# Key loads ahead of the weights, two clamps on VectorE, and the last tokens' product at the end of kv's accumulation

## The chip, the core and the metric

The kernel runs on one core of a Trainium2 chip. The metric is the device time of one execution in microseconds (us). Before the change it is 1074.74 us, the median of three runs (1074.12 to 1076.08). The engines have short names: PE is TensorE (matmuls; PEld its weight loads), DVE is VectorE, ACT is ScalarE, POOL is GpSimd, and SP only issues transfers. Each engine works through its own instructions strictly in the order in which they were written to it.

## The reference

An attention with random features, and a feed-forward product over its output:

```python
q_s, k_s = (q * scale, k * scale)
def phi(x):
    h = einsum('bhsd,md->bhsm', x, omega) - sum(x * x) / 2.0
    return np.exp(h - max(h)) / np.sqrt(m)
q_p, k_p = (phi(q_s), phi(k_s))
kv = einsum('bhsm,bhsd->bhmd', k_p, v);  z = sum(k_p, axis=2)
attn = einsum('bhsm,bhmd->bhsd', q_p, kv) / (einsum('bhsm,bhm->bhs', q_p, z) + 1e-06)
x = attn, heads side by side              # 4608 tokens x 512
h = x @ w_in                              # 512 x 2048
out = (h - np.tanh(h)) @ w_out            # 2048 x 512
```

There are 8 batches, 8 heads, 576 tokens, a head size of 64 and 128 features.

## The kernel before

**Units.** The heads go in four pairs c (0 to 3). A *k unit* (b, c) turns the keys of batch b into features and sums them with the values to `kv` and z. A *q unit* (ch, c) turns a chunk of 256 tokens of queries into the transposed attention output x. Batches 0 and 1 and chunks 0 to 2 are done "native" in f32, with tiles of the pool a0; this is the first stage. A native `k_unit` loads `kf` (keys) and `v` (values) through SP, lets POOL copy the last 64 tokens of both heads into the diagonal blocks `kd` and `vd` (L186, L187), and makes features on PE (L160, L196), their smallest exponents on DVE (L162, L197) and the exponentials on ACT (L164, L198). Then PE accumulates kv in `pk`: first the product of the last tokens (`ph`, `vd`, L201), then eight products over the other 512 tokens (L205). z goes to DVE (L212) and, transposed, to `zb`, which the q units read.

**Weights.** `w` holds both weight matrices as f64 words, in 16 slices f of 1 MB. `fetch` loads a slice into `raw`; `decode` splits it into two fp32r parts: absolute value on ACT (L437), a middle word `m` on ACT (L439), a clamp on POOL (L440), bit work on DVE (L442, L443, L446), the high part on ACT (L450), and two more DVE operations (L451, L452) that give `w`. The tile `a` has two buffers and `m` one, so the `m` of a slice waits for L452 of the slice before. The first 10 slices have places of their own; the places of slices 10 to 15 lie where a0 lay, so their loads wait for the end of the first stage.

**Feed-forward.** Chunks 0 and 1 run together: `step(s)` takes hidden slice s, with 12 matmuls of `ffn_h` into one of two PSUM banks `h0`, `h1` (L469), tanh on ACT (L473), `g` on DVE (L474, which frees the bank), `gh` on ACT (L475) and `gl` on DVE (L476), and then 12 matmuls of `ffn_out` of the step before (L487 to L489). From chunk 2 on the loop at the end of the function does the same by chunk, with the units of later batches between the steps; those units use two PSUM banks `pj` in turn.

**Order.** The loop `while decoded < NF` counts ticks t: it fetches and decodes by t, starts units by the table `start`, and begins step s once slice s + 2 is decoded. A scheduler then orders each engine's instructions by times that it works out itself, so what stands where on an engine is read from the built program. All loads of the first stage go through SP in one chain.

Of the kernel before, what the change touches and what calls it, by code (L numbers as in the profile page):

```python
# [8 lines left out]
F32 = mybir.dt.float32  # L9
# [5 lines left out]
ALU = mybir.AluOpType  # L15
# [10 lines left out]
E = D + 2  # L26
# [5 lines left out]
def favor_attention_ffn(ctx: ExitStack, tc: tile.TileContext, qT, kT, va, vt, omT, w, out):  # L32
# [12 lines left out]
    nc = tc.nc  # L45
# [12 lines left out]
    def close_pool(name):  # L58
        pools.pop(name).__exit__(None, None, None)
# [4 lines left out]
    def bank(kind):  # L64
        tags = mode[kind]
        tags.append(tags.pop(0))
        return tags[-1]

    def att(kind, shape, dtype, name):
        pool, bufs = mode[kind]  # L70
        return pool.tile(shape, dtype, tag=kind, name=name, bufs=bufs)
# [7 lines left out]
    def load(dst, src):  # L79

        i = nc.sync.dma_start(dst, src)
        if mode.get("chain"):
            tc.keep_in_program_order(i)
# [69 lines left out]
    def features_f(f, toks, name):  # L153

        n = 2 * len(toks)
        ph = att("phi", [P, 4, M], F32, f"phi_{name}")
        nb = sb.tile([P, 4], F32, tag="nb", name=f"nb_{name}", bufs=12)
        pj = ps.tile([P, 4, M], F32, tag=bank("pj"), name=f"pj_{name}")
        for i, (a, b) in enumerate(toks):
            nc.tensor.matmul(pj[:, 2 * i : 2 * i + 2].rearrange("p a m -> p (a m)"), f[:, a:b],  # L160
                             om_bd.rearrange("p a m -> p (a m)"), start=True, stop=True)
        nc.vector.tensor_reduce(nb[:, :n], pj[:, :n], axis=AX.X, op=ALU.min)  # L162
        for j in range(n):
            nc.scalar.activation(ph[:, j], pj[:, j], AF.Exp, bias=nb[:, j : j + 1], scale=-1.0)  # L164
        return ph
# [4 lines left out]
    def k_unit(b, c):  # L170

        n = f"{b}_{c}"
        if not mode["native"]:
            f = att("kf", [P, S], F32, f"kf_{n}")
            load(f, kT[c, :, b * S : (b + 1) * S])
            yield from k_single(b, c, f)
            return
        f = att("kf", [P, S], F32, f"kf_{n}")
        load(f, kT[c, :, b * S : (b + 1) * S])
        if (b, c) == (0, 0):  # L180
            fetch(0)
        v, kd, vd = bank("v")
        load(v[:, :, 0:D], va[b, c])
        for h in range(2):
            r = slice(h * D, h * D + D)
            nc.gpsimd.tensor_copy(kd[r, r], f[r, 4 * P : S])  # L186
            nc.gpsimd.tensor_copy(vd[r, h], v[r, 4])  # L187
        yield
        phs = []
        for t in range(0, 4, 2):  # L190
            phs.append(features_f(f, [(t * P, t * P + P), (t * P + P, t * P + 2 * P)], f"k{t}_{n}"))
            yield
        ph = att("ph5", [P, M], F32, f"ph5_{n}")
        nb = sb.tile([P, 4], F32, tag="nb", name=f"nb5_{n}", bufs=12)
        pj = ps.tile([P, M], F32, tag=bank("pj"), name=f"pj5_{n}")
        nc.tensor.matmul(pj, kd, oms, start=True, stop=True)  # L196
        nc.vector.tensor_reduce(nb[:, 0:1], pj, axis=AX.X, op=ALU.min)  # L197
        nc.scalar.activation(ph, pj, AF.Exp, bias=nb[:, 0:1], scale=-1.0)  # L198
        yield
        pk = ps.tile([P, 512], F32, tag=bank("pk"), name=f"pk_{n}")  # L200
        nc.tensor.matmul(pk[:, 0 : 2 * E], ph, vd.rearrange("p h e -> p (h e)"),  # L201
                         start=True, stop=False)
        for h in range(2):
            for t in range(4):
                nc.tensor.matmul(pk[:, E * h : E * h + E], phs[t // 2][:, 2 * (t % 2) + h],  # L205
                                 v[:, 5 * h + t], start=False, stop=(h, t) == (1, 3))
            if h == 0:
                yield

        pkh = pk[:, 0 : 2 * E].rearrange("p (h x) -> p h x", h=2)  # L210
        z = sb.tile([P, 2], F32, tag="z", name=f"z_{n}", bufs=4)
        nc.vector.tensor_copy(z, pkh[:, :, D])  # L212
        w = None
        if b > 0:
            w = att("kvw", [P, 4, D], F32R, f"kvw_{n}")
            nc.scalar.copy(w[:, 0::3, :], pkh[:, :, 0:D])
            nc.vector.tensor_sub(w[:, 1:3, :], pkh[:, :, 0:D], w[:, 0::3, :].bitcast(F32))
            w = w.rearrange("p a d -> p (a d)")
        for h in range(2):
            nc.scalar.copy(kvf[b][c][:, h, D * h : D * h + D], pkh[:, h, 0:D])  # L220
        yield
        for h in range(2):
            nc.tensor.transpose(pk[:, 256 + 128 * h : 384 + 128 * h],
                                z[:, h : h + 1].to_broadcast([P, P]), ident)
        zb = att("zb0" if b == 0 else "zb", [P, 2, M], F32, f"zb_{n}")
        nc.scalar.copy(zb.rearrange("p h m -> p (h m)"), pk[:, 256:512])
        kvs[b, c] = (w, zb)
# [186 lines left out]
    raws = {}  # L414
    places = {}

    def weight_places(pool, fs):
        for f in fs:
            places[f] = pool

    def fetch(f):
        if f in places and f not in raws:
            raws[f] = places[f].tile([P, 2 * DM], U64, tag=f"w{f}", name=f"raw{f}")
            load(raws[f], w[f])

    def decode(f):


        top = raws[f].bitcast(U32)[:, 1::2]
        topf = raws[f].bitcast(F32)[:, 1::2]  # L430
        mid = raws[f].bitcast(U16)[:, 1::4]
        a = dec.tile([P, 2 * DM], U32, tag="a", name=f"a{f}", bufs=2)
        m = dec.tile([P, 2 * DM], U32, tag="m", name=f"m{f}", bufs=1)

        nc.scalar.activation(a.bitcast(F32), topf, AF.Abs)  # L437

        nc.scalar.activation(m, mid, AF.Copy, scale=128.0)  # L439
        nc.gpsimd.tensor_scalar(a.bitcast(F32), a.bitcast(F32), 2.0**-15, 122879.9921875,  # L440
                                op0=ALU.max, op1=ALU.min)
        nc.vector.tensor_scalar(a, a, 3, 0x3FFFF000, op0=ALU.logical_shift_left, op1=ALU.bitwise_and)  # L442
        nc.vector.scalar_tensor_tensor(out=a, in0=top, scalar=0xC0000000, in1=a,  # L443
                                       op0=ALU.bitwise_and, op1=ALU.bitwise_or)

        nc.vector.scalar_tensor_tensor(out=m, in0=top, scalar=23, in1=m,  # L446
                                       op0=ALU.logical_shift_left, op1=ALU.bitwise_or)

        wt[f] = places[f].tile([P, 2, 2 * DM], F32R, tag=f"w{f}", name=f"w{f}")
        nc.scalar.copy(wt[f][:, 0], a.bitcast(F32))  # L450
        nc.vector.tensor_scalar(a, a, 0xFF800000, None, op0=ALU.bitwise_and)  # L451
        nc.vector.scalar_tensor_tensor(out=wt[f][:, 1], in0=m, scalar=2.0**-43, in1=a.bitcast(F32),  # L452
                                       op0=ALU.mult, op1=ALU.mult)
# [78 lines left out]
    mode["v"] = kv_tiles(a0, (0, 1, 2))  # L532
    start = {}
    for c in range(NC):
        start.setdefault(2 * c, []).append(("k", 0, c))
        for i in range(2):
            start.setdefault(2 * c + 5 + 2 * i, []).append(("q", i, c))
        start.setdefault(8 + 2 * c, []).append(("k", 1, c))
        start.setdefault(14 + 2 * c, []).append(("q", 2, c))
    t = decoded = done = 0  # L540
# [10 lines left out]
        prev = g  # L551

    while decoded < NF:
        if t == 1:
            fetch(1)
        if not gens and not start and len(places) < NF:
            close_pool("a0")
            weight_places(open_pool("w1", "left"), range(10, NF))
            for f in range(decoded, decoded + 2):
                fetch(f)  # L560
        if decoded in raws and t >= 1 + 3 * min(decoded, 16) + 2 * max(0, decoded - 16):
            decode(decoded)
            decoded += 1
            fetch(decoded + 2 - 1)
        if t == 15:
            mode.update(pj=["pj0", "pj1", "po1"], pk=["pk"], pt=["pt", "po0"])
        if done + 2 < decoded and t >= 23 + 1 * done:
            if done == 0:
                assert xdone[0] == xdone[1] == NC
                out_tiles(0, ("po0", "po1", "pj1", "pt"))  # L570
                mode.update(pj=["pj0"], pk=["pk"], pt=["pk"])
            step(done)
            done += 1
        tick(start.pop(t, ()))
        t += 1
# [12 lines left out]
    start = {}  # L588
    for ch in range(3, NCH):
        for c in range(NC):  # L590
            k = 28 + 4 * c if ch == 3 else 42 + 4 * c if ch == 4 else 16 * (ch - 1) - 6 + 4 * c
            start.setdefault(k, []).append(("q", ch, c))
    for b in range(2, B):
        for c in range(NC):
            k = 31 + 5 * c if b == 2 else 16 * (need[b] - 1) - 25 + 8 * c
            start.setdefault(k, []).append(("k", b, c))
    t = 32 - 2 * (NF - done)
# [67 lines left out]
```

## Time and profile before

| what | value |
|---|---|
| median of 3 runs | 1074.74 us |
| the profiled execution's own time | 1074.43 us |
| its span, first to last instruction | 1072.6 us |
| mean granted PE clock | 0.989 |
| PE busy | 1045.6 us (97%) |
| DVE busy | 853.1 us (80%) |
| ACT busy | 713.4 us (67%) |
| POOL busy | 328.5 us (31%) |

The view of windows gives for stretches of the span how long each engine was busy (with the number of its instructions), the clock that PE was granted as a share of full speed, the share of the transfer engines and what they moved. The view of waits lists who waited for whom. In the timeline a row holds the start, the length, engine, line, operation, output and input tiles, and in brackets the idle time ahead of it with what ended it. DVE starts its next instruction a little before the row of the last one ends, so what an instruction costs there is read from start to start.

### The profile page before, as it was taken

To read this page: it belongs to the slowest core of one execution; us is meant where nothing else is said; L and a number is where in the kernel's file an instruction comes from. 1 tells how busy PE (TensorE), PEld (TensorE's weight loads), DVE (VectorE), ACT (ScalarE), POOL (GpSimd) and SP (SyncE) were. 2 spreads that over 40 slices of the span, in tenths; PEclk is the share of its full clock that TensorE was granted. 3 is DMA by queue.
4 is the path that set the end of the run, shared out by engine and by line. 5 is a ranking of instruction groups with operands and counts; after the bars stand their busy time and mean duration, and the time that the engine had idled before them with its cause. 6 is when DMAs were issued, how large, how long until landed. Compare 5 with 4: busy or idle time off the path is not lost. (4 is left out here: it accounts for less than half of the span.)

```text
span 1072.6 us, 20340 instructions
## 1 busy us (share of the span) xinstructions
PE 1045.6 (97%) x6760; PEld 951.3 (89%) x6760; DVE 853.1 (80%) x3028; ACT 713.4 (67%) x1833; POOL 328.5 (31%) x555
## 2 busy tenths in 40 slices
PE   6888999998999999999999999999999999999998
PEld 5777888997999999999999999999999999999997
DVE  5999796898888986688888888898888897666522
ACT  5997565777777765577777766777767775555422
POOL 8534440344433320133333333233333331000000
PEclk8999999998999999999999999999999999999999
DMA  9651401111111110011111111111101110000000
GB/s 296 175 179 60 189 1 36 58 28 53 33 53 33 53 33 30 12 53 33 52 34 43 43 28 53 31 45 33 53 22 52 29 42 11 30 11 26 1 21 20
DMA packets 35530, 55.91 MB, mean 52 GB/s; under 512 B 12256, under 2 KB 21600, under 8 KB 33376
## 3 DMA queue, kind: packets, MB, share of 16 engines
q1 hardware_dynamic: 35344, 54.57, 16.1%
q8 instruction: 54, 0.88, 0.3%
q14 instruction: 52, 0.43, 0.1%
q10 hardware_dynamic: 80, 0.03, 0.0%
HBM read 45.15 MB, written 9.44 MB: 51 GB/s over the span
## 5 line engine op out<-in xcount | busy, mean ns | idle before, releaser
L469 PE MATMUL h<-xh,w 128*128 128x256 f32 (+1 forms) x2176 | 454.2, 292 | 2.1 <-DVE g L474 2.1
L469 PEld LDWEIGHTS h<-xh,w 128*128 128x128 f32 x2176 | 357.1, 191 | 12.0 <-DVE g L474 2.7
L469 PE MATMUL h<-xl,w 128*128 128x256 f32 (+1 forms) x1088 | 317.2, 292 | 0.5 <-DVE xl L409 0.5
L487 PE MATMUL po<-w,gh 128*128 128x512 f32 x544 | 214.1, 394 | 0.0
L469 PEld LDWEIGHTS h<-xl,w 128*128 128x128 f32 x1088 | 207.8, 191 | 6.6 <-DVE xl L409 0.8
L488 PE MATMUL po<-w,gh 128*128 128x512 f32 x544 | 213.7, 393 | 0.0
L489 PE MATMUL po<-w,gl 128*128 128x512 f32 x544 | 210.1, 392 | 0.0
L473 ACT ACTIVATE g<-h 128x512 f32<-128x512 f32 x144 | 85.0, 590 | 96.5 <-PE h L469 89.8
L474 DVE TENSOR_TENSOR g<-h,g 128x512 f32<-128x512 f32 x144 | 98.8, 686 | 60.8 <-ACT g L473 60.0
L475 ACT CAST gh<-g 128x512 fp32r<-128x512 f32 x144 | 89.5, 621 | 85.8 <-DVE g L474 83.4
L476 DVE TENSOR_TENSOR gl<-g,gh 128x512 fp32r<-128x512 f32 x144 | 109.4, 760 | 42.1 <-ACT gh L475 38.7
L489 PEld LDWEIGHTS po<-w,gl 128*128 128x128 f32 x544 | 102.1, 188 | 20.4
L487 PEld LDWEIGHTS po<-w,gh 128*128 128x128 f32 x544 | 102.6, 189 | 16.6 <-ACT gh L475 0.2
L488 PEld LDWEIGHTS po<-w,gh 128*128 128x128 f32 x544 | 102.5, 188 | 15.2
L349 DVE CUSTOM_DVE_ANT_0 junk<-phi_q,zb 128x128 f32<-128x128 f32 (+1 forms) x320 | 95.9, 303 | 14.7 <-ACT phi_q L150 0.8
L252 POOL TENSOR_TENSOR khl<-phi_ka,khl 128x256 fp32r<-128x256 f32 x48 | 38.3, 799 | 155.3 <-DVE khl L251 134.1
L440 POOL TENSOR_SCALAR a<-a 128x1024 f32<-128x1024 f32 x16 | 62.1, 3883 | 67.6 <-ACT a L437 55.7
L150 ACT ACTIVATE phi_q<-phi_q,nb_q 128x128 f32<-128x128 f32 x240 | 79.1, 392 | 4.7 <-DVE nb_q L146 4.5
L260 POOL CAST vhl<-v 128x128 fp32r<-128x128 f32 (+1 forms) x144 | 44.6, 311 | 103.1 <-PE pk L268 78.6
L389 DVE TENSOR_TENSOR ql<-pt,qh 128x512 fp32r<-128x512 f32 x60 | 41.1, 685 | 27.5 <-ACT qh L388 27.2
L146 DVE CUSTOM_DVE_ANT_0 phi_q<-pj_q,phi_q 128x128 f32<-128x128 f32 x240 | 55.8, 283 | 2.8 <-ACT phi_q L143 2.5
L261 DVE TENSOR_TENSOR vhl<-v,vhl 128x128 fp32r<-128x128 f32 (+1 forms) x144 | 44.7, 311 | 16.3 <-POOL vhl L260 12.8
(150 smaller groups left out, 1961.0 us busy)
## 6 DMA issues: line engine op xcount, KB each, us to landing
raw<-w SPq DMA_DIRECT2D x16, 1024.0 KB, 7.2
kf<-kT SPq DMA_DIRECT2D x32, 288.0 KB, 2.9
qf<-qT SPq DMA_DIRECT2D x72, 128.0 KB, 2.1
out<-o SPq DMA_DIRECT2D x36, 256.0 KB, 2.0
v<-vt SPq DMA_DIRECT2D x24, 288.0 KB, 2.9
v<-va SPq DMA_DIRECT2D x8, 288.0 KB, 5.9
omf<-omT ACTq DMA_DIRECT2D x1, 32.0 KB, 2.1
omf<-omT SPq DMA_DIRECT2D x1, 32.0 KB, 2.3
```

The lines of the kernel that those rows point to most:

```text
L146: nc.vector.tensor_tensor_reduce(ph[:, j], pj[:, i, :M], ph[:, j], scale=-SCALE, scalar=3.0e38, op0=ALU.add, op1=ALU.min, accum_out=nb[:, ...
L150: nc.scalar.activation(ph[:, j], ph[:, j], AF.Exp, bias=nb[:, j : j + 1], scale=-1.0)
L349: nc.vector.tensor_tensor_reduce(bank("junk")[r], ph[r, i], kvs[b, c][1][r, h], scale=1.0, scalar=EPS, op0=ALU.mult, op1=ALU.add, accum_ou ...
L440: nc.gpsimd.tensor_scalar(a.bitcast(F32), a.bitcast(F32), 2.0**-15, 122879.9921875, op0=ALU.max, op1=ALU.min)
L469: nc.tensor.matmul(o, w_, x, start=i == 0, stop=i == len(prods) - 1)
L473: nc.scalar.activation(g, p, AF.Tanh)
L474: nc.vector.tensor_sub(g, p, g)
L475: nc.scalar.copy(gh, g)
L476: nc.vector.tensor_sub(gl, g, gh.bitcast(F32))
L487: nc.tensor.matmul(po[t], h, wt[f][:, 0, DM:], start=first, stop=False)
L488: nc.tensor.matmul(po[t], h, wt[f][:, 1, DM:], start=False, stop=False)
L489: nc.tensor.matmul(po[t], l, wt[f][:, 0, DM:], start=False, stop=last)
```

## The change

The first k units start at ticks 0, 1, 3 and 5 (before 0, 2, 4, 6). Slice 0 is no longer fetched inside the first k unit, and slices 0 and 1 are fetched at ticks 2 and 4. Decodes are due at tick 4 + 2.5 f (before 1 + 3 f). The clamp of slices 0 and 1 runs on VectorE. In native k units the product of the last tokens closes the accumulation of `pk`.

```diff
@@ k_unit
         load(f, kT[c, :, b * S : (b + 1) * S])
-        if (b, c) == (0, 0):
-            fetch(0)
         v, kd, vd = bank("v")
@@
-        nc.tensor.matmul(pk[:, 0 : 2 * E], ph, vd.rearrange("p h e -> p (h e)"),
-                         start=True, stop=False)
         for h in range(2):
             for t in range(4):
                 nc.tensor.matmul(pk[:, E * h : E * h + E], phs[t // 2][:, 2 * (t % 2) + h],
-                                 v[:, 5 * h + t], start=False, stop=(h, t) == (1, 3))
+                                 v[:, 5 * h + t], start=(h, t) == (0, 0), stop=False)
             if h == 0:
                 yield
+        nc.tensor.matmul(pk[:, 0 : 2 * E], ph, vd.rearrange("p h e -> p (h e)"),
+                         start=False, stop=True)
@@ decode
-        nc.gpsimd.tensor_scalar(a.bitcast(F32), a.bitcast(F32), 2.0**-15, 122879.9921875,
-                                op0=ALU.max, op1=ALU.min)
+        engine = nc.vector if f < 2 else nc.gpsimd
+        engine.tensor_scalar(a.bitcast(F32), a.bitcast(F32), 2.0**-15, 122879.9921875,
+                             op0=ALU.max, op1=ALU.min)
@@ favor_attention_ffn
-        start.setdefault(2 * c, []).append(("k", 0, c))
+        start.setdefault([0,1,3,5][c], []).append(("k", 0, c))
@@
-        if t == 1:
-            fetch(1)
+        if t in (2, 4):
+            fetch(int(t == 4))
@@
-        if decoded in raws and t >= 1 + 3 * min(decoded, 16) + 2 * max(0, decoded - 16):
+        if decoded in raws and t >= 4 + 2.5 * min(decoded, 16) + 2 * max(0, decoded - 16):
             decode(decoded)
```

What this does to the engines' orders is shown at three places. (Lines of the changed kernel have other numbers: L439 is its clamp, L441, L442, L445, L450 and L451 its other DVE operations of a decode, L473 and L475 its `g` and `gl`.) Numbers at the end of a name are buffers; `a8` is slice 8's, `kf_0_1` that of batch 0 and pair 1.

First, SP at the start of the program. Before:

```order
L81 DMA kf_0_0_140<-kT 128x576
L81 DMA raw0_142<-w 128x1024
L81 DMA v0_122<-va 128x9x64
L81 DMA raw1_149<-w 128x1024
L81 DMA raw2_163<-w 128x1024
L81 DMA kf_0_1_185<-kT 128x576
L81 DMA v1_125<-va 128x9x64
```

and in the changed kernel:

```order
L81 DMA kf_0_0_140<-kT 128x576
L81 DMA v0_122<-va 128x9x64
L81 DMA kf_0_1_157<-kT 128x576
L81 DMA v1_125<-va 128x9x64
L81 DMA raw0_164<-w 128x1024
L81 DMA kf_0_2_202<-kT 128x576
L81 DMA v2_128<-va 128x9x64
L81 DMA raw1_209<-w 128x1024
```

Keys and values of two units moved ahead of all weights, those of the third ahead of slice 1.

Second, POOL after its memsets. Before:

```order
L186 COPY kd0_123<-kf_0_0_140 64x64 x2
L440 TENSOR_SCALAR a0_151<-a0_151 128x1024
L187 COPY vd0_124<-v0_122 64x66 x2
L440 TENSOR_SCALAR a1_208<-a1_208 128x1024
L186 COPY kd1_126<-kf_0_1_185 64x64 x2
```

and in the changed kernel:

```order
L184 COPY kd0_123<-kf_0_0_140 64x64 x2
L185 COPY vd0_124<-v0_122 64x66 x2
L184 COPY kd1_126<-kf_0_1_157 64x64 x2
L185 COPY vd1_127<-v1_125 64x66 x2
L184 COPY kd2_129<-kf_0_2_202 64x64 x2
```

Two clamps left this queue; the copies follow each other.

Third, DVE just ahead of `g_0_1`, the `g` of step 1 (the rows of L349 are a q unit's denominators). Before:

```order
L443 SCALAR_TENSOR_TENSOR a8_1159<-raw8_988,a8_1159 128x1024
L446 SCALAR_TENSOR_TENSOR m8_1160<-raw8_988,m8_1160 128x1024
L349 ISA junk1_105,dn_2_3_1060<-phi_q2_3_1050,zb_1_3_1032 128x128
L349 ISA dn_2_3_1060 128x1
L349 ISA junk_65,dn_2_3_1060<-phi_q2_3_1050,zb_1_3_1032 64x128
L349 ISA dn_2_3_1060 64x1
L474 TENSOR_TENSOR g_0_1_1140<-h_0_1_1127,g_0_1_1140 128x512
```

and in the changed kernel:

```order
L442 SCALAR_TENSOR_TENSOR a7_1072<-raw7_908,a7_1072 128x1024
L347 ISA junk1_105,dn_2_3_1060<-phi_q2_3_1050,zb_1_3_1032 128x128
L347 ISA dn_2_3_1060 128x1
L347 ISA junk_65,dn_2_3_1060<-phi_q2_3_1050,zb_1_3_1032 64x128
L347 ISA dn_2_3_1060 64x1
L445 SCALAR_TENSOR_TENSOR m7_1073<-raw7_908,m7_1073 128x1024
L473 TENSOR_TENSOR g_0_1_1154<-h_0_1_1141,g_0_1_1154 128x512
```

At the same step DVE is one slice further back in decoding: slice 8 was in work there before, slice 7 is now. Counted over the whole program up to `g_0_1`, DVE has two clamps more than before (slices 0 and 1), and five operations fewer: L451 and L452 of slice 7, and L442, L443 and L446 of slice 8 (lines of before). Everything else ahead of it is the same work in another order. Ahead of `g_0_3` the count is two clamps more against L451 and L452 of slice 9.

## The prediction

> **What bounds the kernel now.** First the windows: the span cut into stretches, to see which engine is full where.
>
> ```profile
> 0.00:10.00 10.00, 6.00 (x26) 5.30 (x26) 2.26 (x6) 3.63 (x5) 6.24 (x30) 1.00 0.77 247
> 10.00:20.00 10.00, 6.25 (x24) 5.81 (x25) 6.70 (x8) 6.47 (x14) 9.74 (x7) 0.61 1.08 364
> 20.00:30.00 10.00, 9.43 (x47) 7.50 (x46) 9.96 (x16) 8.88 (x28) 9.43 (x12) 0.87 0.77 234
> 30.00:40.00 10.00, 7.69 (x45) 5.84 (x43) 8.77 (x27) 8.20 (x25) 4.94 (x6) 1.00 0.58 174
> 40.00:100.00 60.00, 53.72 (x308) 45.72 (x308) 59.50 (x191) 54.74 (x158) 26.77 (x18) 0.97 0.45 147
> 110.00:120.00 10.00, 10.00 (x48) 8.30 (x48) 4.82 (x6) 6.34 (x9) 3.43 (x1) 1.00 0.81 314
> 120.00:160.00 40.00, 40.00 (x179) 33.10 (x178) 36.80 (x41) 23.46 (x30) 18.88 (x6) 1.00 0.12 49
> ```
>
> The busy columns are PE, PEld, DVE, ACT, POOL, and after them PE's granted clock. From 40 to 100 us DVE is busy 59.50 of 60 us, and from 110 on PE 10.00 of 10. So the first stage is bound by DVE and the rest by PE. The change touches only the first stage, so it is worth what it takes from the moment at which PE becomes full. The view of waits and the timeline show that moment:
>
> ```profile
> PE pk L201 <- POOL vd L187: 6.0, 1, 6.0
> PE h L469 <- DVE g L474: 2.1, 2, 1.8
> PE pj_kb L142 <- DVE nb_km L146: 1.8, 1, 1.8
> ...
> 97.64 4.05 POOL L440 TENSOR_SCALAR a<-a 128x1024 f32<-128x1024 f32 x1 [5.10 <-ACT a L437]
> 98.12 2.06 DVE L446 SCALAR_TENSOR_TENSOR m<-raw,m 128x1024 uint32<-128x1024 uint32 x1
> ...
> 100.75 0.69 DVE L474 TENSOR_TENSOR g<-h,g 128x512 f32<-128x512 f32 x1
> ...
> 101.36 0.17 DVE L352 RECIPROCAL dn<-dn 128x4 f32<-128x4 f32 x1
> ...
> 101.50 0.50 PE L469 MATMUL h<-xh,w 128*128 128x512 f32 x1 [1.81 <-DVE g L474]
> ...
> 187.80 0.39 PE L469 MATMUL h<-xh,w 128*128 128x256 f32 x1 [0.28 <-DVE g L474]
> ```
>
> The L474 row is `g_0_1`; it frees the bank for the matmuls of step 3, which start at 101.50. Between that wait and the last row, at 187.80, PE waits for nothing. **The end is therefore the end of `g_0_1` plus a fixed remainder of PE work**, as long as nothing new waits behind it. The remainder is the same in the changed kernel: the same steps and the same three parts of the last q unit stand behind step 3.
>
> **Step 1: fewer decode operations ahead of `g_0_1`.** Counted in the two orders, the changed DVE has two clamps more ahead of it, and L451, L452 of slice 7 and L442, L443, L446 of slice 8 fewer. What these cost on a full DVE is read from start to start:
>
> ```profile
> 59.44 0.68 DVE L162 TENSOR_REDUCE nb_k<-pj_k 128x4 f32<-128x512 f32 x1
> 60.04 0.68 DVE L451 TENSOR_SCALAR a<-a 128x1024 uint32<-128x1024 uint32 x1
> 60.64 0.41 DVE L409 TENSOR_TENSOR xl<-pn,xh 128x256 fp32r<-128x256 f32 x1
> ...
> 61.46 1.22 DVE L443 SCALAR_TENSOR_TENSOR a<-raw,a 128x1024 uint32<-128x1024 uint32 x1
> 62.59 0.28 DVE L217 TENSOR_TENSOR kvw<-pk,kvw 128x128 fp32r<-128x128 f32 x1
> ```
>
> L451 takes 0.60, and L442 has its shape; L443 takes 1.13, and L446 and L452 have its shape. Gone: 2 x 0.60 + 3 x 1.13 = 4.6 us. No row shows a clamp on DVE. Its nearest row is L451 (the same operation with two constants, size and width, SBUF to SBUF): 0.60; the upper end is L443's 1.13, the lower 0.3, half of L451's. So 1.2 us more (0.6 to 2.3), and **-3.4 us (-4.0 to -2.3)**. The operations come due later, behind `g_0_1`. There DVE has cover: PE next needs a bank for step 4 after step 3's 2.8 us and some 6 us of output matmuls, products and transposes (the three parts of the last q unit now stand ahead of step 4), and DVE's work to `g_0_2` is 6.3 us. By `g_0_3` all but 0.5 us is caught up. From 110 to 160 DVE has 5.2 + 3.2 us to spare. If that cover is gone, the 3.4 us come back one for one.
>
> **Step 2: DVE's idle time at the start.** Before, DVE is idle 7.7 + 3.3 + 0.0 + 1.2 = 12.3 us up to 40. The rows behind this:
>
> ```profile
> 6.70 0.69 DVE L162 TENSOR_REDUCE nb_k<-pj_k 128x4 f32<-128x512 f32 x1 [3.02 <-PE pj_k L160]
> ...
> 7.96 1.12 ACT L437 ACTIVATE a<-raw 128x1024 f32<-128x1024 f32 x1 [5.04 <-DMA raw<-w]
> ...
> 9.24 3.62 POOL L440 TENSOR_SCALAR a<-a 128x1024 f32<-128x1024 f32 x1 [2.81 <-ACT a L437]
> 9.99 2.17 ACT L164 ACTIVATE phi_k<-pj_k,nb_k 128x128 f32<-128x128 f32 x8
> 10.13 1.23 DVE L446 SCALAR_TENSOR_TENSOR m<-raw,m 128x1024 uint32<-128x1024 uint32 x1 [1.68 <-ACT m L439]
> ...
> 12.81 0.88 POOL L187 COPY vd<-v 64x66 f32<-64x66 f32 x2
> 12.89 0.70 DVE L442 TENSOR_SCALAR a<-a 128x1024 uint32<-128x1024 uint32 x1 [1.54 <-POOL a L440]
> ...
> GB/s 32 327 349 419 346 381 291 366 99 161 47 136 371 72 100 246 275 125 269 240 13 339 26 10 228 422 396 3 0 0 0 0 5 0 0 31 378 425 425 355
> ```
>
> PE's 6.0 us wait is POOL's order: the clamp waits for ACT, ACT for slice 0, and the copy of `vd` stands behind the clamp. The changed POOL has no clamp there, and PE asks for `vd` last. The wait goes, but only what DVE gets from it counts. In the changed kernel, the first reduction stays at 6.70, since the first keys still come first. Slice 0 comes later: 4 x 0.29 + 0.06 + 1.05 = 2.3 MB end with it instead of 1.4. In the GB/s row (slices of 3.1 us) 1.4 MB are moved at 7.1 us, 0.85 ahead of L437's start, and 2.3 MB at 9.6; so slice 0 can be used at about 10.4. ACT first makes the exponentials of two k units: 16 at 0.27 (2.17 / 8) and one of 0.3 from 7.4 on, with short waits for the second unit's minima, to 12.1. Then L437 runs, and DVE's first clamp starts at about 13.2. DVE has done 3.6 us of work by then and was idle 9.6; before, it was idle 11.0 up to 12.89. What is late next: slice 1's `m` has one buffer and waits for slice 0's L452 (0.5), the first q unit's denominators wait for their exponentials (0.6), and slice 1's L451 for ACT's copy (0.8). That makes 11.5 against 12.3: **-0.8 us (-3 to +2**: the lower end is the 6.0 us wait halved, the upper one slice load of 2.5 us late at the first clamp). The third unit's copies on POOL and the loads of slices 1 and 2 hide beside this.
>
> **Step 3: clamps beside DVE.** L446 at 98.12 began beside a clamp and took 2.06 us; at 10.13, also beside one, 1.23. One clamp fewer on POOL runs beside the full DVE up to `g_0_1` (slices 2 to 8, before 2 to 9), at 0 to 0.83 us: **-0.4 us**. The Trainium skill (SBUF — State Buffer, section "SBUF: two separate sides") says that the ports that VectorE and GpSimd share are an exclusive lock, so that the second to start blocks fully. By that rule the L446 at 98.12 would have waited for the clamp's end at 101.69, and a clamp fewer would be worth up to 3.6 us; the two rows say 0.83 at most, and the sum goes by them.
>
> **Step 4: the later units.** After 187 us the orders differ only by small swaps. One bears on the wait `pj_kb` <- `nb_km`: the three scalings (L358) of the next q unit now stand ahead of that `nb_km`. Two of them and what follows, at a place where DVE is full:
>
> ```profile
> 64.53 0.47 DVE L358 TENSOR_SCALAR phi_q<-phi_q,dn 128x128 f32<-128x128 f32 x2
> 64.92 0.28 DVE L349 CUSTOM_DVE_ANT_0 junk<-phi_q,zb 128x128 f32<-128x128 f32 x1
> ```
>
> Two take 0.39, so 0.2 us each: **+0.6 us (0, if they fall into idle time, to 1.1, if each costs nearly double)**.
>
> The sum is -3.4 - 0.8 - 0.4 + 0.6 = -4.0 us. The profiled execution took 1074.43 us (span 1072.6 and 1.8 around it), 0.3 under the median, so both give about **1070.4 us**.
>
> **Rivals.** The price of PE's clock decides two of them. It halves after waits, and these rows show what that costs:
>
> ```profile
> 12.00:13.00 1.00, 0.00 (x0) 0.00 (x0) 0.11 (x1) 1.00 (x3) 1.00 (x2) 0.65 0.99 413
> ...
> 22.00:23.00 1.00, 1.00 (x6) 0.79 (x4) 1.00 (x4) 1.00 (x4) 1.00 (x1) 0.73 1.17 328
> ...
> 241.57:255.35 13.78, 10.36 (x47) 9.12 (x46) 12.88 (x55) 10.88 (x32) 6.98 (x15) 0.63 0.32 100
> 255.35:262.00 6.65, 6.65 (x48) 6.19 (x47) 6.02 (x27) 4.96 (x14) 1.63 (x4) 1.00 0.00 1
> ```
>
> The 6.0 us wait brought 10 us of half clock (12.65 to 22.7). The waits around 243 us (1.8 the longest) brought another 10, and 47 matmuls took 13.78 us where the next 48 took 6.65: 7 us. The wait of 1.81 at 101.5 brought none. The Trainium skill (TensorE: Matmul & The Clock Gate, section "HAM oscillation — how this bites in real kernels") names idle gaps above about 3.4 us as what halves the clock. By that rule the waits at 243 would cost 3 us and not 7; the trace does not agree.
>
> - **The waits at 243 us shrink** below what halves the clock, because DVE meets PE there in another phase. DVE's work up to that `nb_km` is within 0.1 us of before by my count, and the L358 rows speak against it. Price -7, to about 1063.5. Chance 0.15.
> - **The early gain is eaten.** PE is busy 53.72 of 60 us and ACT 54.74 from 40 to 100, so they may not follow a faster DVE, and step 1 is then no gate. Only steps 2 to 4 remain, halved: 1073 to 1076, say 1074. Chance 0.2.
> - **Slower: decoding comes due too late.** These rows show slice 10:
>
> ```profile
> 110.27 0.93 PE L373 MATMUL pn<-qt,kvf 128*128 128x64 f32 x6
> ...
> 113.00:114.00 1.00, 1.00 (x6) 0.79 (x5) 0.38 (x1) 0.59 (x1) 0.00 (x0) 1.00 0.98 410
> ...
> 115.34 1.14 ACT L437 ACTIVATE a<-raw 128x1024 f32<-128x1024 f32 x1
> ...
> 116.57 7.72 POOL L440 TENSOR_SCALAR a<-a 128x1024 f32<-128x1024 f32 x2 [14.88 <-ACT a L437]
> ```
>
>   Its load starts when the last product of the first stage (the L373 row) is out, at about 112, and its clamp ends near 120.4. In the changed DVE order its three bit operations stand ahead of `gl_0_4`, before they stood behind. If the clamp ends over 21 us behind `g_0_1`, PE waits; I expect 16 to 17 (19 before, with the last product 2.7 us earlier now). Past that point each us costs one, and the first such wait of 2 us halves the clock for 10 us: 5 more. Together with step 1's 3.4 handed back: 1070.4 + 3.4 + 2 + 5 = 1081, and about 1078 where only a part comes. Chance 0.1.
> - **The change does nothing**: only if the clamp on DVE costs several us; L451's row excludes it.
>
> **How the numbers follow.** Forecast -4.0 with its bounds (1068 to 1072.5): 0.55. The range reaches from the shrunken waits to a little above the eaten gain: 1062.5 to 1075.5. About 0.2% (2.1 us) is what a measurement of this kernel can tell from no change. Faster by more: 0.55 and 0.15, less a little at the edge, and a little of the second rival: 0.69. Within: 0.2. Slower: 0.11.
>
> **What would show it.** Right: `g_0_1` ends near 97 us; the first DVE clamp starts near 13 and lasts 0.6 to 0.7; PE's 6.0 us wait for `vd` is gone; PE is full from there to 187 less 4; the half clock near 240 is still there. Wrong: `g_0_1` later than 99; a wait of PE for `gl` or `w` between 100 and 160; a second stretch of half clock, or none, past 180.

## The result and the profile after

| | kernel before | changed kernel |
|---|---|---|
| median, us | 1076.18 (6 runs, 1074.12 to 1076.63) | 1069.95 (6 runs, 1069.50 to 1071.79) |
| ratio, 95% interval | 1 | 0.9950 (0.9937 to 0.9963) |
| span of the profiled execution, us | 1072.6 | 1068.2 |
| mean granted PE clock | 0.989 | 0.991 |

The change makes the kernel 0.5% faster, 4.0 to 6.8 us by the interval, 6.2 us by the two medians and 4.4 us by the two profiled spans; the forecast was 4.0 us, to 1070.4. (A trace is one execution: that of before, 1074.43 us, is one of its faster ones, those of undo_ticks and undo_clamp below, 1081.78 and 1079.02 us, are their slowest.) What follows accounts for the 4.4 us between the two traces; why the medians lie 1.8 us further apart, the traces kept do not show.

First the windows of the changed kernel, with the columns of the prediction (PE, PEld, DVE, ACT and POOL busy, PE's clock):

```profile
0.00:10.00 10.00, 7.83 (x36) 7.00 (x37) 3.81 (x7) 3.77 (x10) 6.85 (x35) 1.00 0.74 207
10.00:20.00 10.00, 7.45 (x53) 6.65 (x51) 7.42 (x15) 8.41 (x22) 1.54 (x4) 0.94 1.09 368
20.00:30.00 10.00, 9.52 (x41) 8.40 (x42) 8.85 (x20) 7.53 (x23) 7.21 (x5) 0.72 0.72 215
30.00:40.00 10.00, 9.41 (x53) 7.71 (x53) 10.00 (x24) 9.89 (x30) 7.40 (x10) 1.00 0.72 211
40.00:100.00 60.00, 50.89 (x277) 41.33 (x278) 59.41 (x194) 51.89 (x144) 22.74 (x13) 1.00 0.42 151
110.00:120.00 10.00, 10.00 (x46) 8.28 (x45) 8.83 (x11) 6.43 (x8) 7.33 (x2) 1.00 0.83 340
```

DVE is as full from 40 to 100 as before (59.41 of 60 us). From 110 to 120 it now works 8.83 us where it worked 4.82: the deferred decode operations were taken up there. Next the timeline, at the places that the prediction named:

```profile
6.64 0.69 DVE L162 TENSOR_REDUCE nb_k<-pj_k 128x4 f32<-128x512 f32 x1 [1.77 <-PE pj_k L160]
13.57 0.69 DVE L439 TENSOR_SCALAR a<-a 128x1024 f32<-128x1024 f32 x1 [0.53 <-ACT a L435]
14.29 0.69 DVE L441 TENSOR_SCALAR a<-a 128x1024 uint32<-128x1024 uint32 x1
...
59.66 4.47 POOL L439 TENSOR_SCALAR a<-a 128x1024 f32<-128x1024 f32 x1 [7.33 <-ACT a L435]
60.56 1.25 DVE L356 TENSOR_SCALAR phi_q<-phi_q,dn 128x128 f32<-128x128 f32 x2
...
93.54 4.17 POOL L439 TENSOR_SCALAR a<-a 128x1024 f32<-128x1024 f32 x1 [2.46 <-ACT a L435]
94.14 1.12 DVE L347 CUSTOM_DVE_ANT_0 junk<-phi_q,zb 128x128 f32<-128x128 f32 x1
...
96.78 0.68 DVE L473 TENSOR_TENSOR g<-h,g 128x512 f32<-128x512 f32 x1
97.52 0.50 PE L468 MATMUL h<-xh,w 128*128 128x512 f32 x1 [1.06 <-DVE g L473]
```

The first clamp on DVE starts at 13.57 (forecast 13.2) and costs 0.72 to the next start. `g_0_1` starts at 96.78 and DVE goes on at 97.38, 3.98 us before the 101.36 of before; PE starts step 3 at 97.52 instead of 101.50 and has no further wait up to 236 us. The two rows beside clamps on POOL (1.25 us for two scalings, 1.12 us for an operation that takes 0.29 elsewhere) matter below.

DVE's work between the first reduction and the end of `g_0_1` stands in one row of windows for each kernel; before:

```profile
6.70:101.36 94.66, 78.14 (x426) 65.62 (x424) 87.81 (x247) 81.48 (x223) 53.01 (x40) 0.93 0.58 187
```

and after:

```profile
6.70:97.39 90.69, 77.61 (x426) 64.44 (x424) 85.10 (x245) 77.95 (x219) 39.75 (x36) 0.96 0.59 200
```

DVE is busy 87.81 and 85.10 us: 2.71 less. It is idle 6.85 and 5.59 us: 1.26 less, nearly all of it ahead of 40 us. Together that is the gain of 3.97 us, and what follows `g_0_1` lasts 971.2 and 970.8 us. In the view of waits the 6.0 us for `vd` are gone, and one wait has grown:

```profile
PE pj_kb L142 <- DVE nb_km L146: 2.8, 1, 2.8
PE h L468 <- DVE g L473: 2.1, 2, 1.1
```

### The profile page after: what moved, and what is told of

The parts are those of the page before. It is cut to its first block, busy times and chain, and to the rows that moved or that the text cites. A ratio compares the mean times of both kernels' runs of the same rounds, so it can differ in the third digit from the quotient of the medians.

```text
span 1068.2 us, 20318 instructions
## 1 busy us (share of the span) xinstructions
PE 1044.0 (98%) x6760; PEld 949.3 (89%) x6760; DVE 854.0 (80%) x3030; ACT 713.2 (67%) x1833; POOL 323.5 (30%) x553
## 5 line engine op out<-in xcount | busy, mean ns | idle before, releaser
L473 DVE TENSOR_TENSOR g<-h,g 128x512 f32<-128x512 f32 x144 | 98.8, 686 | 66.4 <-ACT g L472 65.3
L475 DVE TENSOR_TENSOR gl<-g,gh 128x512 fp32r<-128x512 f32 x144 | 109.9, 764 | 38.3 <-ACT gh L474 36.5
L439 POOL TENSOR_SCALAR a<-a 128x1024 f32<-128x1024 f32 x14 | 59.0, 4214 | 54.7 <-ACT a L435 42.1
```

Source lines behind the costliest of these rows:

```text
L439: engine.tensor_scalar(a.bitcast(F32), a.bitcast(F32), 2.0**-15, 122879.9921875, op0=ALU.max, op1=ALU.min)
L473: nc.vector.tensor_sub(g, p, g)
L475: nc.vector.tensor_sub(gl, g, gh.bitcast(F32))
```

## The experiments

All runs in one table. "rest" is the span less the end of `g_0_1` (the start of the `g` row plus 0.61); DVE's busy and idle time are counted from 6.70 us to that end. These four columns come from one trace each, the medians from all runs of a kernel.

One thing must be known for reading these columns. In seven of the fourteen traces (undo_ticks, undo_clamp, dve_early, before_vd_last, before_defer, clamp_dve and x_first_kv) PE gets going late: its first eight products take 3.78 us instead of 1.99. Two kernels that are the same up to 230 us show what this is worth in the changed order: `g_0_1` ends at 97.22 us in x_first and at 98.22 in x_first_kv. So where a microsecond counts, traces that begin alike are compared; those of before and of the changed kernel both have the 1.99.

| kernel | `g_0_1` ends | DVE busy | DVE idle | rest | median us | ratio to before (95%) |
|---|---|---|---|---|---|---|
| before | 101.36 | 87.81 | 6.85 | 971.2 | 1076.18 | 1 |
| changed | 97.39 | 85.10 | 5.59 | 970.8 | 1069.95 | 0.9950 (0.9937 to 0.9963) |
| undo_ticks | 109.20 | 88.99 | 13.51 | 970.7 | 1078.40 | 1.0017 (1.0006 to 1.0029) |
| undo_clamp | 102.88 | 85.23 | 10.95 | 974.3 | 1077.97 | 1.0000 (0.9983 to 1.0017) |
| undo_loads | 102.16 | 90.85 | 4.61 | 969.9 | 1075.52 | 0.9995 (0.9982 to 1.0008) |
| undo_vd | 101.08 | 86.56 | 7.82 | 970.7 | 1072.29 | 0.9962 (0.9946 to 0.9978) |
| clamp_pool | 105.12 | 84.14 | 14.28 | 969.9 | 1077.18 | 1.0005 (0.9996 to 1.0015) |
| dve_early | 104.13 | 90.41 | 7.02 | 971.4 | 1077.43 | 1.0014 (1.0005 to 1.0023) |
| dve_behind | 97.05 | 85.12 | 5.23 | 977.4 | 1077.92 | 1.0017 (1.0007 to 1.0027) |
| before_vd_last | 101.77 | 87.68 | 7.39 | 975.0 | 1077.48 | 1.0013 (1.0001 to 1.0024) |
| before_defer | 99.00 | 84.59 | 7.71 | 978.2 | 1078.91 | 1.0019 (1.0009 to 1.0028) |
| clamp_dve | 98.36 | 85.05 | 6.61 | 970.9 | 1071.05 | 0.9959 (0.9944 to 0.9974) |
| x_first | 97.22 | 85.22 | 5.30 | 969.8 | 1068.81 | 0.9928 (0.9915 to 0.9942) |
| x_first_kv | 98.22 | 85.25 | 6.27 | 967.5 | 1067.81 | 0.9923 (0.9911 to 0.9935) |

### One part undone at a time

Each of these four takes one part of the change back (the part of the diff in "The change", reversed) and leaves the order to the scheduler.

> The changed kernel with the decode due times of before (1 + 3 f instead of 4 + 2.5 f). In the order of VectorE two bit operations of 0.60 and two of three scalings more stand ahead of g_0_1, one product for w less is left out; by the spacings of the prediction that is 3.0 us more VectorE work ahead of g_0_1. Theory A (the end is the end of g_0_1, and that is the VectorE work ahead of it plus its idle time): g_0_1 ends near 100.4 us instead of 97.4, and the whole takes about 1073, 3 more than the changed kernel. Rival B (the gain comes from the start: keys first, no wait for vd): g_0_1 stays within 1 us of 97.4 and the time within 1 us of 1070.

> The changed kernel with the clamps of slices 0 and 1 back on GpSimd. VectorE has 0.6 us less work ahead of g_0_1 by the order, but the first clamp takes 3.6 us on GpSimd instead of 0.7. Theory A: what counts is whether VectorE has other work in the 3.6 us; it has the second and third unit's reductions only, so its idle time rises by about 2 us each for the two slices, less 0.6: g_0_1 ends 1 to 3 us later than 97.4, time 1071 to 1073. Rival B (where the clamp stands matters nothing, since GpSimd is idle at the start now): g_0_1 ends 0.6 us earlier, time 1069.5.

> The changed kernel with the order of loads and the start of the k units as before. By the order, VectorE has 4.8 us more work ahead of g_0_1 (slices 7 and 8 of the decode back ahead of it). Theory A: the slices come at the time of before, the clamps on VectorE cut its idle time by some 2 us, so g_0_1 ends near 100 to 102 and the time is 1073 to 1075. Rival B (the start alone makes the gain, and the clamp and the order of products give most of it): under 1071.

> The changed kernel with the product of the last tokens first again in kv's accumulation. GpSimd's copies of vd end at 7.0 us there, ahead of the first exponentials, so TensorE should not wait for vd. By the order, VectorE has 1.2 us more work ahead of g_0_1. Theory A: g_0_1 ends about 1.2 us later than 97.4, time near 1071. Rival B (the order of the products is a main part of the change): TensorE waits for ph, whose exponential comes last, instead of vd; 3 us or more are lost and the time is above 1073.

In each, `g_0_1` ends later and the median is longer: rival B falls for the ticks, the loads and the clamp, and undo_vd (2.3 us slower, 1.2 expected; its interval overlaps that of the changed kernel) is nearest to theory A. But the sizes are off, and only in undo_loads is PE's last wait still the one for `g_0_1` (rest 969.9 us); in undo_ticks it is for the `x` of a q unit, in undo_clamp for `g_0_0`, in undo_vd for `gl`. undo_ticks was to cost 3 us and costs 8.4 by the medians. In its trace DVE has 3.9 us more work, and 7.9 us more idle time. One wait of PE and two windows of undo_ticks show where from:

```profile
PE pj L194 <- POOL kd L184: 2.6, 1, 2.6
```

```profile
30.00:40.00 10.00, 7.20 (x24) 5.93 (x24) 9.79 (x26) 8.26 (x25) 7.33 (x10) 0.54 0.16 37
40.00:100.00 60.00, 52.98 (x266) 44.14 (x266) 54.79 (x184) 48.96 (x146) 19.78 (x16) 0.88 0.51 167
```

PE's clock is halved there for 13.7 us and, behind another wait, for 10.2 us, and DVE idles 5.2 us between 40 and 100, 3.4 of them waiting for PE. The scheduler moved much besides the part that was undone (what the four lose adds up to 24 us, far more than the whole change gains). So they show that the order that it finds without the ticks, the loads or the clamp loses the whole gain, not what a part is worth. From here on the order of every engine is held: a table in the kernel chains each engine's instructions in the order of the changed kernel (or of the one before), and only the rows named are edited.

### DVE work added ahead of `g_0_1`, and behind it

```diff
-        nc.vector.tensor_scalar(a, a, 0xFF800000, None, op0=ALU.bitwise_and)
+        for _ in range(7 if f == 5 else 1): nc.vector.tensor_scalar(a, a, 0xFF800000, None, op0=ALU.bitwise_and)
```

For dve_behind it is `f == 7`.

> The changed kernel with every engine's order held to that of the changed kernel, and the masking operation of slice 5 (128x1024, 0.60 us) done seven times instead of once, so that VectorE has 3.6 us more work some 30 us ahead of g_0_1. Theory A (g_0_1 is where VectorE's work ends, and the rest is a fixed remainder): g_0_1 ends 3.6 us later, near 101, and the time rises by 3.6 to about 1073.6. Rival B (TensorE and ScalarE set the pace there too, VectorE has slack): g_0_1 moves by less than 1.5 us and the time by as much.

> The same 3.6 us of extra masking, in slice 7, that is directly behind g_0_1 in VectorE's order, where the change put the decode operations that it deferred; all orders held. Theory A (there is cover behind g_0_1): g_0_1 stays near 97.4. The trace has 2.5 us between the end of g_0_2 and its use by TensorE and 1.1 us at g_0_3, and VectorE idles 1.4 us between them, so of the 3.6 us some 1.2 us show: time near 1071.2. Rival B (deferred work comes back one for one): 1073.6. Rival C (all of it hidden): 1070.

The timeline of dve_early has the added work and its first victim:

```profile
79.72 5.05 DVE L450 TENSOR_SCALAR a<-a 128x1024 uint32<-128x1024 uint32 x7
86.25 1.09 PE L363 MATMUL pt<-ident,phi_q 128*128 128x128 f32 x4 [4.47 <-DVE phi_q L356]
...
91.56 4.60 POOL L439 TENSOR_SCALAR a<-a 128x1024 f32<-128x1024 f32 x1 [15.41 <-DVE dn L347]
94.39 0.69 DVE L473 TENSOR_TENSOR g<-h,g 128x512 f32<-128x512 f32 x1 [0.56 <-ACT g L472]
95.33 1.37 DVE L450 TENSOR_SCALAR a<-a 128x1024 uint32<-128x1024 uint32 x1 [0.24 <-ACT w L449]
```

Seven take 5.05 us, so 4.3 were added (0.72 each: an operation that reads what the last one wrote costs more than the 0.60 of a mixed stream). `g_0_1` comes 6.7 us later than in the changed kernel, and 5.9 later than in x_first_kv, whose trace also has the 3.78. Of these 5.9, 5.16 are more work of DVE (the 4.3, and a masking operation that took 1.37 instead of 0.69 beside a clamp) and 0.75 more idle time: the block had held PE up for 4.47 us and PE's clock was halved for 6.8 us. DVE is the gate (rival B falls), and work in one block cost more than its length.

In dve_behind `g_0_1` is where it was (97.05), and the rest is 6.6 us longer:

```profile
105.10 0.73 PE L488 MATMUL po<-w,gl 128*128 128x512 f32 x2 [2.37 <-DVE gl L475]
107.67 2.50 PE L371 MATMUL pn<-qt,kvf 128*128 128x64 f32 x8 [1.60 <-ACT qt L366]
```

I had read the slack from `g_0_2` and `g_0_3` and overlooked `gl_0_1`, which ends at 100.92 in the changed kernel and is asked for at 101.06. PE waited 2.37 and 1.60 us and ran at half clock for 6.8 us. So rival B's direction is right: directly behind `g_0_1` there is no cover left.

### The deferral alone, and the order of products alone

Both in the held order of the kernel before. In before_defer DVE's order is

```diff
-L443 SCALAR_TENSOR_TENSOR a8<-raw8,a8 128x1024
-L446 SCALAR_TENSOR_TENSOR m8<-raw8,m8 128x1024
 ...
 L474 TENSOR_TENSOR g_0_1<-h_0_1,g_0_1 128x512
 ...
-L451 TENSOR_SCALAR a8<-a8 128x1024
 L476 TENSOR_TENSOR gl_0_1<-g_0_1,gh_0_1 128x512
+L443 SCALAR_TENSOR_TENSOR a8<-raw8,a8 128x1024
+L446 SCALAR_TENSOR_TENSOR m8<-raw8,m8 128x1024
+L451 TENSOR_SCALAR a8<-a8 128x1024
```

and `w8`'s high copy on ACT goes behind `gh_0_1`. In before_vd_last the eight products with `vd` (L201) follow the eight products with `v` instead of leading them.

> The kernel before, all orders held, with two bit operations of slice 8 (the second ones of a and m, 128x1024, 1.13 us each, one of them stretched to 2.06) moved on VectorE from ahead of g_0_1 to behind gl_0_1, and the high copy of that slice on ScalarE to behind gh_0_1. Nothing is changed at the start of the program. Theory A (what is deferred past g_0_1 is gained, as far as TensorE waits there, 1.8 us): g_0_1 ends 2 to 2.7 us earlier, TensorE's products of step 3 start near 99.7 instead of 101.5, and the deferred work costs at most 0.5 us at g_0_2; the time is 1.3 to 1.8 us under the kernel before. Rival B (there is no cover behind g_0_1, as the run dve_behind suggests): g_0_1 is as early, but TensorE waits for g_0_2 or gl as long instead, and the time is not below the kernel before, or above it if that wait halves the clock.

> The kernel before, all orders held, with the one edit that in native k units the product of the last tokens closes the accumulation instead of opening it. TensorE's 6.0 us wait for the copy of vd should go or shrink to the wait for the first exponentials. Theory A (only what VectorE gets counts; VectorE's waits at 10.13 and 12.89 are for ScalarE and GpSimd): g_0_1 ends within 1 us of 101.4, and the time stays within 1.2 us of the kernel before. Rival B (the wait and the half clock behind it delay the first stage): 3 to 6 us faster, near the changed kernel.

before_defer brings `g_0_1` forward by 2.4 us and loses more at the next step:

```profile
104.62 0.69 DVE L451 TENSOR_SCALAR a<-a 128x1024 uint32<-128x1024 uint32 x1 [1.17 <-ACT w L450]
108.10 0.69 DVE L474 TENSOR_TENSOR g<-h,g 128x512 f32<-128x512 f32 x1
108.84 0.74 PE L469 MATMUL h<-xh,w 128*128 128x512 f32 x1 [2.88 <-DVE g L474]
```

`g_0_2` starts at 108.10 (before: 106.04), since the deferred operations and those of slice 9 stand ahead of it, and PE waits 2.88 us with 3.4 us of half clock behind. Rival B holds, for these three operations at this place; one of them, L451, also waited 1.17 us for ACT behind the move. What the change does is more: there slice 9's operations go behind `g_0_2` as well, and the work is handed on from step to step until it meets the 5.2 us that DVE idled between 110 and 120. In before_vd_last the wait is gone and next to nothing is gained:

```profile
13.02 0.70 DVE L442 TENSOR_SCALAR a<-a 128x1024 uint32<-128x1024 uint32 x1 [1.54 <-POOL a L440]
13.87 0.81 PE L207 MATMUL pk<-vd,ph 128*128 128x132 f32 x2 [0.46 <-POOL vd L187]
```

PE waits 0.46 us for `vd`, and DVE the same 1.54 us for the clamp, at 13.02 where it was 12.89; `g_0_1` ends at 101.77. PE's late start in this trace, 0.86 us at the first reduction, has shrunk to 0.13 there, so it hides no gain of any size. Theory A holds: the longest wait in the list was worth next to nothing, since DVE did not wait for what stood behind it. (The rest of 975.0 us has 3.4 us of half clock behind `g_0_1`.)

### The clamp

clamp_pool puts the clamps of slices 0 and 1 alone back on POOL, clamp_dve moves those of slices 2 to 8 to DVE too (`f < 9`), each ahead of its L441; all else is held.

> The changed kernel, all other orders held, with the clamps of slices 0 and 1 alone back on GpSimd, behind the copies of vd of the second and of the third unit. VectorE saves two operations of 0.72 us and waits for two of 3.6 us instead, at 14.3 and 19.8 us of the changed kernel's trace. Theory A (VectorE's idle time at the start goes into the end one for one): the first costs 2.9 us, the second up to as much less the 1.2 us that VectorE idles behind it anyway, so g_0_1 ends 3 to 5 us later than 97.4 and the time is 1073 to 1075. Rival B (there is slack between the start and g_0_1): g_0_1 within 1 us, time near 1070.

> The changed kernel, all other orders held, with the clamps of slices 2 to 8 on VectorE too, each directly ahead of its shift-and-mask. VectorE gets six clamps of 0.72 us ahead of g_0_1, 4.3 us; GpSimd's clamps are gone there. Theory A (each clamp on GpSimd holds one VectorE operation up once, by 0.6 to 0.84 us, as the seven long VectorE rows beside the seven clamps in the changed kernel's trace say, 4.6 us together): g_0_1 ends within 1 us of 97.4. Rival B (0.4 us for each clamp, as the prediction took it): 1.5 to 2 us later. Rival C (GpSimd costs VectorE nothing, long rows are chance): 4.3 us later.

In clamp_pool DVE waits twice:

```profile
17.06 0.70 DVE L441 TENSOR_SCALAR a<-a 128x1024 uint32<-128x1024 uint32 x1 [4.30 <-POOL a L439]
25.83 0.69 DVE L441 TENSOR_SCALAR a<-a 128x1024 uint32<-128x1024 uint32 x1 [4.30 <-POOL a L439]
```

DVE works 0.96 us less and idles 8.7 more: theory A's direction, but `g_0_1` is 7.7 us later and the time 7.2 us longer instead of 3 to 5. In clamp_dve, with six more clamps ahead of `g_0_1`, DVE is busy 85.05 us, where it was busy 85.10 without them. The two long rows of the changed kernel shown above, at 60.56 and 94.14, are short again:

```profile
62.46 0.47 DVE L356 TENSOR_SCALAR phi_q<-phi_q,dn 128x128 f32<-128x128 f32 x2
95.96 0.28 DVE L347 CUSTOM_DVE_ANT_0 junk<-phi_q,zb 128x128 f32<-128x128 f32 x1
```

Laid side by side up to `g_0_1`, the two orders of DVE differ by the six clamps alone, and seven operations are shorter in clamp_dve, by 0.36 to 0.84 us and 5.0 us together. Seven clamps stood beside them on POOL in the changed kernel: five had one such row, one two and one none. So a clamp on POOL cost DVE about 0.7 us, as much as a clamp on DVE (0.72). `g_0_1` ends 0.97 us later than in the changed kernel and 0.14 later than in x_first_kv, whose trace has the 3.78 too: theory A. The Trainium skill (SBUF — State Buffer, section "SBUF: two separate sides") lets the first of the two hold the shared ports for its whole instruction while the other blocks; these clamps last 3.6 to 4.6 us and held a DVE operation up by at most 0.84, and the measurement decides.

### The waits near 240 us

x_first edits one place of the changed kernel's order. On ACT (the rows' old places, further on, are left out):

```diff
 L150 ACTIVATE phi_q4_0<-phi_q4_0,nb_q4_0 128x128
+L143 COPY phi_km2_2<-pj_km2_2_0 128x128
+L307 COPY kvs_2_1<-pk_2_1 128x128
+L397 COPY tmp_3_3<-pn_3_3 64x256
+L398 COPY tmp_3_3<-pn_3_3 64x256
 L499 COPY o_2_0<-po0_2 128x512
+L406 CAST xh<-xs_3_3 128x256
 L354 ACTIVATE phi_q4_0<-phi_q4_0,dn_4_0 128x128
```

On DVE `nb_km`, `xs_3_3` and `xl` go ahead of the scalings L356 of `phi_q4_0` likewise, and on PE 13 products `h_3` go behind the second pair of `pj_kb`. In x_first_kv four products of kv (L266) are put ahead of all or all but two of these 13.

> The changed kernel, all orders held but for one place near 236 us. There TensorE waits 2.8 us for nb_km and soon 1.2, 0.6 and 0.5 us more, and its clock is halved from 241 to 251. Moved ahead: on ScalarE the copies of phi_km, kvs_2_1 and tmp_3_3 and the cast of xh from xs_3_3 go ahead of a scaling that waits for VectorE; on VectorE nb_km, xs_3_3 and xl go ahead of the three scalings of phi_q; on TensorE 13 products h_3 that wait for that x go ahead of the kv products. Theory A (the wait and the halved clock behind it are lost time, since TensorE is the bound from 97 us on): the wait shrinks to about 1.5 us in all, no half clock follows, and the time falls by 3.4 us of waits and up to 4 of clock, 4 to 7 us, to 1063 to 1066. Rival B (VectorE, busy 93% from 230 to 260, is the bound there): the wait only moves to a later place, and the time stays within 2 us of 1070. Rival C (the wait shrinks but the clock is halved all the same): 1066 to 1068.

> The kernel of x_first, with the four kv products of that place on TensorE no longer behind the 13 products h_3: two of them directly behind the pair of pj_kb, the other two behind the first two products h_3. In x_first VectorE waited 1.61 us for them (and 0.45 for GpSimd behind), at a place where VectorE is busy nearly all of the time. Theory A (VectorE is the bound between 236 and 252 us, so TensorE's halved clock and its waits there cost little, and an idle time of VectorE costs all of its length): 1 to 2 us faster than x_first, near 1067.3. Rival B (TensorE is the bound there; the kv products only change places): within 0.5 us of x_first, 1068.8.

(The 93% of the first expectation is the figure of the kernel before; in the changed one DVE is busy 26.57 of the 30 us, 89%.) The windows of the changed kernel there:

```profile
230.00:240.00 10.00, 7.18 (x49) 6.47 (x49) 9.01 (x40) 6.61 (x21) 3.15 (x6) 1.00 0.12 39
240.00:250.00 10.00, 7.75 (x34) 6.64 (x33) 9.25 (x31) 7.62 (x21) 5.51 (x13) 0.54 0.30 87
250.00:260.00 10.00, 10.00 (x72) 9.47 (x71) 8.31 (x35) 6.95 (x20) 2.83 (x5) 0.95 0.05 13
```

of x_first:

```profile
230.00:240.00 10.00, 7.74 (x50) 6.61 (x49) 9.46 (x40) 8.12 (x25) 3.36 (x6) 1.00 0.12 42
240.00:250.00 10.00, 8.32 (x52) 7.41 (x53) 7.75 (x31) 6.79 (x19) 5.41 (x13) 0.83 0.27 85
250.00:260.00 10.00, 8.86 (x60) 8.01 (x59) 9.61 (x38) 7.23 (x20) 3.91 (x7) 1.00 0.05 15
```

and its timeline:

```profile
238.73 0.50 PE L468 MATMUL h<-xh,w 128*128 128x256 f32 x2 [1.38 <-ACT xh L406]
242.38 0.23 DVE L249 CAST khl<-phi_km 128x128 fp32r<-128x128 f32 x1 [1.61 <-PE pk L266]
252.04 0.39 PE L468 MATMUL h<-xh,w 128*128 128x256 f32 x1 [1.14 <-DVE g L473]
```

The wait of 2.8 us shrank to 0.28 and the half clock from 10.2 to 3.4 us, and the time fell by 1.1 us only. PE's waits had moved: 1.38 us for `xh` at 238.73, 1.14 for `g` at 252, and in sum PE is idle 5.1 us from 230 to 260 in both kernels. DVE lost 1.61 us at 242.38, waiting for the kv products that I had put behind the others. With these back ahead (x_first_kv) DVE has no such wait, 9.37 of 10 us are busy from 240 to 250, PE's idle time falls to 3.65 us, and another 1.0 us is gained. The intervals of the two overlap, but their rests, 969.8 and 967.5 us against 970.8 in the changed kernel, say the same. That is what rival B of x_first and theory A of x_first_kv forecast, so at this place DVE sets the pace; as PE's waits fell with DVE's in the second run, the two are not wholly told apart. x_first_kv, at 1067.81 us, is 2.1 us under the changed kernel and the fastest of all; its interval against before (0.9911 to 0.9935) ends just below where that of the changed kernel begins.

## Why the prediction was right

- **What bounds the kernel: right.** "The end is the end of `g_0_1` plus a fixed remainder": the remainder is 971.2 and 970.8 us, and 969.9 to 971.4 in undo_loads, clamp_pool, dve_early and clamp_dve, though `g_0_1` ends between 98.4 and 105.1 there. Where it was longer (975 to 978), a new wait or a half clock came behind `g_0_1`. (In undo_ticks, undo_clamp and undo_vd PE did not wait for `g_0_1`, so their rests prove nothing here.)
- **Step 1, -3.4 us: right, nearly in size.** The clamps cost 0.72 instead of 0.6, so -3.15 is what the order gives. That the deferral is gained is shown by the whole change only; before_defer shows that the cover which I named behind `g_0_1` is not there for two or three operations alone. That the step holds because the order hands the work on behind `g_0_2` is read from the trace, and no run tries it. "One for one" where the cover is gone was too low: dve_behind paid 6.6 us for 4.3.
- **Step 2, -0.8 us: right in kind, too small.** DVE's idle time fell by 1.26 us. That the 6.0 us wait itself counts for next to nothing is shown by before_vd_last.
- **Step 3, -0.4 us: wrong, and of the wrong sign.** Busy time fell by 2.71 where step 1 alone gives 3.15, so the stretched rows took 0.4 us more instead of less. I had priced a clamp beside DVE from two L446 rows, one of them free; clamp_dve gives about 0.7 for each, and one clamp fewer did not mean fewer rows drawn out.
- **Step 4, +0.6 us: not told apart.** The 19th row of `g` (191.06 against 195.12) is 4.06 us ahead of before, the 61st (496.71 against 500.61) 3.90, and the spans end 4.4 apart: a loss of 0.2 at the most, then a gain of 0.5 that no run explains.
- **The rivals.** The waits near 240 grew to 2.8 us instead of shrinking, and the half clock of 10 us stayed. Its price of 7 us was too high as far as tried: the term counted PE's loss at a place where DVE, busy 12.88 of 13.78 us in the prediction's own row, would have held PE up anyway. x_first took 6.8 of the 10.2 us of half clock away for 1.1 us, and x_first_kv 1.4 us of waits besides for 2.1. The early gain was not eaten (PE started step 3 3.98 us earlier). Slice 10 came in time: its clamp ends 16.3 us behind `g_0_1`, as expected.

The sum met the result because its misses nearly cancel: +0.25, -0.46 and +0.84 in steps 1 to 3 (`g_0_1` 3.97 us earlier, forecast 4.6) and -1.0 behind `g_0_1` (0.4 less, forecast 0.6 more). The total is better than its terms, and that is luck. So is how near the time itself came: 1070.4 was reckoned from an execution of 1074.43, and from the later median of before, 1076.18, the same 4.0 us would have led to 1072.2.

## What to carry to other kernels

Find the engine that sets the moment from which the bound engine never waits, and price an edit by that engine's busy and idle time up to that moment; a long wait elsewhere, even with a halved clock behind it, may be worth nothing. Deferred work is gained only if every later due time, down to small ones like `gl`, still has slack, so follow it until it meets idle time. A wait of PE of some 2 us may bring half clock behind it (3.4 to 13.7 us in these traces); price that too, but only where PE is the bound. And before a difference of a microsecond between two traces is explained, look whether both began alike.

## What the runs showed of the hardware

- Stretches of half clock in these traces last 3.4, 6.8, 10.2 or 13.7 us, multiples of 3.41. The Trainium skill (TensorE: Matmul & The Clock Gate, section "What's actually happening") states a free-running window of 3413 ns, which the multiples agree with. The limit of about 3.4 us of idle time, which the prediction quoted from it, is too wide here: waits of 1.8 to 2.9 us halved the clock (1.79 near 244 us before, 2.88 in before_defer), and 1.81 at 101.5 did not. In the 3.41 us ahead of these two falls (up to 244.40 and 108.93) PE was busy 1.26 and 0.53 us; in the 3.41 us up to 101.04, 2.06 us. No sharp limit shows: the clock also fell in before_vd_last behind such a stretch with 2.64 us busy, and stayed full in before behind one with 1.57 (up to 39.60).
- The same first eight products on PE, from the same place in the program, took 1.99 us in the trace of before and 3.78 us in that of before_vd_last:

```profile
5.53 1.99 PE L160 MATMUL pj_k<-om_bd,kf 128*128 128x256 f32 x8 [0.70 <-POOL om_bd L109]
5.45 3.78 PE L160 MATMUL pj_k<-om_bd,kf 128*128 128x256 f32 x8 [0.62 <-POOL om_bd L109]
```

  The view of windows gives a clock of 1.00 for both, but that is no reading: the records of the clock begin at 5.46 us in the first trace and at 10.34 in the second, and ahead of its first record the view prints 1.00. In the seven traces with 1.99 the records begin 4.2 to 5.5 us behind the span's start, in the seven with 3.78 9.2 to 10.4 us behind it. So the longer products fit a half clock that lasts some 5 us longer at the start, an estimate from those times. What decides between the two starts was not tried; of two kernels that are the same up to 230 us, x_first showed the one and x_first_kv the other.
- A clamp of 3.6 to 4.6 us on POOL cost a full DVE about 0.7 us, mostly through one drawn-out operation (seven clamps, 5.0 us).
